# Moving lays to ScalarE, a third row rectified ahead, fp32 dummies and an earlier weight slot in an attention and spectral-mixing kernel

## The chip, the cores and the metric

The kernel runs on one core of a Trainium2 chip. The metric is the device time of one execution in microseconds, the median of several runs. The profile is of one execution, taken by the hardware profiler; its times are in microseconds from the start of the span. The engines are PE (TensorE matmuls), PEld (TensorE weight loads), DVE (VectorE), ACT (ScalarE), POOL (GpSimd) and SP (SyncE, which here only issues the output stores). Transfers run on DMA engines that the profile shows as one mean share.

## The reference

The input is q, k, v of shape (8 batches, 8 heads, 576 positions, 64), 64 pairs of weight matrices w_r and w_i of 512 x 512, one for each Fourier mode, and one matrix w_ch of 512 x 512.

```python
scores = q @ k.T / sqrt(64), masked to 0 <= pos_q - pos_k < 64
x = softmax(scores) @ v                       # per batch: 576 x 512
X = rfft(x, axis=seq)[:, :64]                 # 64 modes are kept
Y[m] = X[m] @ (w_r[m] + 1j * w_i[m])          # complex, per mode
u = x + irfft(Y, n=576)
out = u + relu(u @ w_ch)                      # fp32, 8 x 576 x 512
```

## The kernel before

The work has three stages, one after another, and beneath them one stream of weight loads.

**Attention** (36 steps of a loop over w, lines 417 to 457). At the start TensorE runs dummy matmuls (`warm_up`, line 369, bf16 128x512 on a tile of zeros) between the first transposes. Each batch's q, k and v are loaded raw, transposed on TensorE in twelve units (`transpose_units`, line 205), and attended in windows of 512 columns; the transposed v lies in the one tile `vT`. When a batch is attended, its rows go into `x_sb`, and TensorE makes its 64 Fourier modes (`dft`, `dft_turn`) into `XQ`.

**Modes** (lines 577 to 592 and 725 to 769). For each mode m TensorE multiplies `XQ` with w_r[m] and w_i[m] (lines 545 and 550). The 127 matrices, 512 KB each in bf16, are loaded by GpSimd's queue in order of use (`load_w`, line 110). GpSimd issues a load as soon as a place for it is free: the first 18 go to two weight pools, the next ones (`spare`, line 363) into tiles that attention no longer needs (raw tiles, kT, qT, vt, and, at step w = 36 of the loop, vT), and from then on a place is taken again when the mode that used it is done (`refill_w`, line 504). In the shadow of these loads `channel` (line 561) computes x @ w_ch for each of 36 row tiles into `Z0`. For each batch `spectrum` and `middle_rows` keep two things on up to 128 partitions, one for each real mode component: the mixed modes (`Yb`) and the mixed modes times w_ch (`yw`). The last four modes are done by `last` (line 751), each matrix as it lands, with dummy matmuls (`idle`, line 688, bf16 128x512) in between.

**Output** (lines 776 to 828). The last modes' rows come out of PSUM on ScalarE and VectorE into `yl`, and GpSimd's queue copies 8 rows for each further batch into that batch's `yw` and `Yb` (`send`, line 787). Then come 36 row tiles of 128 rows. Each takes one of eight PSUM banks in turn (`bank`, line 705) and goes through five steps:

1. lay (line 711): TensorE multiplies Z0's tile with the identity, which puts x @ w_ch into the bank;
2. rectify (line 808): TensorE adds the inverse transform of `yw`, ScalarE applies Relu in place;
3. finish (line 812): TensorE adds the inverse transform of `Yb`;
4. VectorE adds x and writes to `ot`;
5. SP issues the store.

The orders of PE, ACT, DVE, POOL and SP in this stage are those of the program text. Row n is rectified two rows ahead of the row being finished and laid four ahead; five rows are laid before the stage. A batch has 4.5 row tiles, so of each pair of batches nine tiles come, and the one with the two half rows (the pair tile) stands last of the nine. It needs two matmuls per add, and two stores.

Of the kernel before, what the change touches and what calls it, by code (L numbers as in the profile page):

```python
# [9 lines left out]
FP32 = mybir.dt.float32  # L10
FP32R = mybir.dt.float32r
BF16 = mybir.dt.bfloat16

ALU = mybir.AluOpType
# [6 lines left out]
def view(ap, off, dims):  # L21

    return bass.AP(ap.tensor, ap.offset + off, [list(ap.ap[0])] + [list(d) for d in dims])
# [3 lines left out]
def kernel(  # L27
# [10 lines left out]
    nc = tc.nc  # L38
    B, H, S, D = q.shape
    NM = moe_w_r.shape[0]  # L40
    DM = moe_w_ch.shape[0]
# [3 lines left out]
    NT = 5  # L45
# [22 lines left out]
    ident_bf = consts.tile([128, 128], BF16, name="ident_bf")  # L68
    ident_r = consts.tile([128, 128], FP32R, name="ident_r")
    x_sb = keep.tile([128, B, NT, DM], BF16, name="x_sb")  # L70
# [48 lines left out]
    warm = acons.tile([128, 512], BF16, name="warm")  # L119
# [29 lines left out]
    with tc.tile_pool(name="tmpf", bufs=1, side="right") as tmp:  # L149
# [8 lines left out]
        for t0, t1 in ((0, 3), (3, NT)):  # L158
            n = t1 - t0
            mt = tmp.tile([128, 2, n * NM], FP32, name="mtf")  # L160
            nc.vector.tensor_tensor(out=view(mt, 0, [[NM, n], [1, NM]]), in0=view(mo, 0, [[0, n], [1, NM]]),
                                    in1=view(to, t0, [[1, n], [0, NM]]), op=ALU.mult)
# [6 lines left out]
    vtp = p1.enter_context(tc.tile_pool(name="vtp", bufs=1, side="right"))  # L169
# [25 lines left out]
    pss = [ps_sc.tile([128, 512], FP32, name=f"pss{i}") for i in range(3)]  # L195
# [167 lines left out]
    def spare(t):  # L363

        nonlocal nw
        load_w(nw, None, None, view(t, 0, [[DM, NC], [1, DM]]))
        nw += 1

    def warm_up(n):
        for _ in range(n):  # L370
            nc.tensor.matmul(out=pss[2], lhsT=warm[:, 0:128], rhs=warm, start=True, stop=True)  # L371

    NU = 12

# [14 lines left out]
    dfts, turns = [], []  # L389
    NWIN = B * H * S // (2 * WIN)  # L390
    with tc.manual_schedule(engines={mybir.EngineType.PE, mybir.EngineType.Pool}):
        warm_up(14)
        first = transpose_units(0)
        for i, j in enumerate((0, 1, 2, 6, 7, 8, 3, 4, 5, 9, 10, 11)):
            first[j]()
            refill(0, j)
            if i in (2, 5):
                warm_up(6)
            if i in (6, 7, 8):
                warm_up(3)  # L400
        sched = {}

        for b in range(1, B):
            start = -(-9 * (b - 1) // 2)

            for i, j in enumerate(range(NU)):
                sched.setdefault(start + i // 3, []).append((b, j))
        units = {}
        mask(0, 1)

        def unit(b, j):
            if b not in units:
                units[b] = transpose_units(b)
            units[b][j]()
            refill(b, j)

        for w in range(NWIN + 1):
            todo = [lambda b=b: dft_turn(b) for b in turns]
            turns[:] = dfts
            todo += [lambda b=b: dft(b) for b in dfts]  # L420
            dfts.clear()
            todo += [lambda b=b, j=j: unit(b, j) for b, j in sched.get(w, [])]
            n = len(todo)
            if w < NWIN:
                scores(w)
            if w:
                cut = closes(w - 1)
                weigh(w - 1, 8 * w - 8, cut)
            if todo:
                todo.pop(0)()  # L430
            if w + 1 < NWIN:
                mask(w + 1, max(1, 3 - n))
            if todo:
                todo.pop(0)()
            if w:
                weigh(w - 1, cut, 8 * w)
            while todo:
                todo.pop(0)()

            if w in (NWIN - 4, NWIN - 1):  # L440
                i = (B - 2) % 2 if w == NWIN - 4 else (B - 1) % 2
                spare(kTs[i])
                spare(qtp.tile([128, 4, S], BF16, name="qT"))
            if w in (NWIN - 4, NWIN):
                i = (B - 2) % 2 if w == NWIN - 4 else (B - 1) % 2
                for j in range(2):
                    spare(vts[i][:, j])
                if w == NWIN - 4:
                    vt_mode = mode_of(nw - 1)
                if w == NWIN:  # L450
                    spare(vtp.tile([128, 4, S], BF16, name="vT"))
        for b in turns:
            dft_turn(b)
        for b in dfts:
            dft(b)
            dft_turn(b)
        early(EARLY)
# [11 lines left out]
    tiles = []  # L469
# [14 lines left out]
    Z0 = late2.tile([128, len(tiles), DM], FP32R, name="Z0")  # L484
    p2d = p2.enter_context(ExitStack())
    ps_a = p2d.enter_context(tc.tile_pool(name="ps_a", bufs=1, space=PSUM, reuse_waits="tile"))
# [69 lines left out]
    with ExitStack() as p2a:  # L556

        def channel_out(i):
            return Z0[:, i, :]
# [17 lines left out]
        for m in range(L0 * MG):  # L577
            mode(m)
            if m == 8:
                for b in range(1, B, 2):  # L580
                    tc.keep_in_program_order(nc.scalar.copy(out=x_sb[64:128, b - 1, NT - 1, :],
                                                            in_=x_sb[64:128, b, NT - 1, :]))
# [9 lines left out]
            if m == Z_M - 2:  # L592

                with tc.tile_pool(name="tmpi", bufs=1, reuse_waits="tile") as tmp:
# [21 lines left out]
                    for tab, row in ((trigI, pcol),):  # L616
# [23 lines left out]
                        for i in range(4):  # L640
# [7 lines left out]
                            for c0, c1, o in ((0, SW, i * SW),) if i < 3 else ((0, 80, 432), (80, SW, 576)):  # L648
                                nc.vector.scalar_tensor_tensor(
                                    out=tab[:, o:o + c1 - c0], in0=mt[:, c0:c1], scalar=coefc,  # L650
                                    in1=tis[:, c0:c1], op0=ALU.mult, op1=ALU.add)
# [33 lines left out]
        nc.vector.tensor_copy(out=pair_tile("Yb", b)[:E0], in_=psa[:E0].rearrange("p c e -> p (c e)"))  # L685
        nc.scalar.copy(out=pair_tile("yw", b)[:E0], in_=psw[:E0, :])

    def idle(n, pool=ps_a, tag="psw"):

        psd = pool.tile([128, DM], FP32, name="psd", tag=tag)  # L690
        for _ in range(n):
            nc.tensor.matmul(out=psd, lhsT=ident_bf, rhs=view(x_sb, 0, [[1, DM]]),
                             start=True, stop=True)

    seq = []
    for b in range(0, B, 2):
        seq += [(b + i, t) for i in range(2) for t in range(NT - 1)] + [(b, NT - 1)]
    NQ = len(seq)
    tps = {}
    taken = 0  # L700
# [4 lines left out]
    def bank(shape, dtype, name):  # L705
        nonlocal taken
        pool, tag = PLACES[taken % len(PLACES)]
        taken += 1
        return pool.tile(shape, dtype, name=name, tag=tag)

    def lay(n):
        ps = tps[n] = bank([128, DM], FP32, "pso8")
        nc.tensor.matmul(out=ps, lhsT=ident_r, rhs=channel_out(tiles.index(seq[n])), start=True, stop=False,  # L713
                         skip_group_check=True)

# [8 lines left out]
    with tc.manual_schedule(engines={mybir.EngineType.PE}):  # L724
        for m in range(M0, ME):
            if (m - M0) % 2 == 0 and (m - M0) // 2 < B // 2:
                b0 = m - M0
                mode(m, lambda: spectrum(b0))
                spectrum(b0 + 1)
            else:  # L730
                mode(m)
            if m == M0 + B - 2:
                wy = late.tile([128, 3, NC, DM], BF16, name="wy", tag="yt")
                free.extend([(wy, j, NM) for j in range(3)])
                refill_w(m)

        YT2 = wlate.tile([128, NC, 96], FP32R, name="YT2", tag="wl")
        nc.vector.tensor_copy(out=YT2[:, :, 0:R - RL], in_=YTl[:, :, 0, 0:R - RL])

        def middle_rows(b0, nb):  # L740
            psa = ps_a.tile([128, NC, 128], FP32R, name="psa", tag="psa")
            psw = ps_a.tile([128, DM], FP32, name="psw", tag="psw")
            turned(lambda e: view(YTl, (e * B + b0) * R, [[1, R * nb]]), R * nb, psa, psw)
            for i in range(nb):
                nc.vector.tensor_copy(out=pair_tile("Yb", b0 + i)[E0:],
                                      in_=psa[R * i:R * i + R].rearrange("p c e -> p (c e)"))
                nc.scalar.copy(out=pair_tile("yw", b0 + i)[E0:], in_=psw[R * i:R * i + R, :])

        psl = ps_l.tile([128, NC, RL * B], FP32, name="psl", tag="psl")

        def last(m, im):
            last_mode(m, wtiles.pop((m, im)), im, 0, NC)

        middle_rows(1, 4)
        last(ME, 0)
        lay(0)
        lay(1)
        last(ME, 1)
        middle_rows(5, 3)
        last(ME + 1, 0)  # L760
        for n in range(2, EARLY_ROWS):
            lay(n)
        idle(4)
        last(ME + 1, 1)
        for m in range(ME + 2, NM):
            for im in range(2):
                idle(6)
                last(m, im)
        idle(2)

    wl.close()
    p3 = p2.enter_context(ExitStack())
# [3 lines left out]
    with tc.manual_schedule(engines={mybir.EngineType.PE, mybir.EngineType.Activation, mybir.EngineType.DVE,  # L776
# [3 lines left out]
        psw = ps_a.tile([128, DM], FP32, name="psw", tag="psw")  # L780
        NR = R + RL * (B - 1)
        turned(lambda e: YT2[:, e, 0:NR], NR, psa, psw)
        idle(2, ps_l, "psl")
        flat = psa.rearrange("p c e -> p (c e)")
        yl = yp.tile([128, 2, DM], FP32R, name="yl")

# [25 lines left out]
        def finish(n):  # L812
            b, t = seq[n]
            add(n, "Yb", True)
            ot = op.tile([128, DM], FP32, name="ot")
            nc.vector.tensor_tensor(out=ot, in0=tps.pop(n), in1=x_sb[:, b, t, :], op=ALU.add)  # L816
            for i, (bb, r0, k) in enumerate(parts_of(b, t)):
                nc.sync.dma_start(out=out[bb, 128 * t:128 * t + k, :], in_=ot[r0:r0 + k, :])

        RELU = 2  # L820
        for n in range(RELU + 1):
            rectify(n)
        for n in range(NQ):
            finish(n)
            if RELU < n + RELU < NQ:
                rectify(n + RELU)
            if EARLY_ROWS <= n + RELU + 2 < NQ:
                lay(n + RELU + 2)


# [28 lines left out]
```

## Time and profile before

| | us |
|---|---|
| median of 4 runs (431.12 to 433.86) | 432.06 |
| profiled execution, its own time | 430.35 |
| span of the profiled execution | 428.6 |
| PE busy | 312.3 (73%) |
| DVE busy | 163.3 (38%) |
| ACT busy | 152.1 (35%) |
| last weight landed, first matmul on it | 391.47 |
| first Relu of the output stage | 395.05 |
| last VectorE sum, start | 422.63 |

The page gives busy shares in forty slices of 10.7 us, so a slice of the three stages can be told apart: attention to about 145 us, modes to about 391, output to the end. Busy shares over the whole span say little here, as the stages have different limits. In the chain of waits each piece of time is put down to the work that the next piece waited for.

### The profile page before, as it was taken

The numbers are of one execution on the slowest core, as the hardware profiler recorded it, in microseconds if no ns is written. First come the engines' busy times: TensorE is split into PE (matmuls) and PEld (weight loads), VectorE is DVE, ScalarE is ACT, GpSimd is POOL, SyncE is SP. The second block draws the span as 40 slices with busy tenths as digits, with TensorE's granted clock in tenths as the row PEclk, the third lists the DMA queues.
The fourth block names the chain that finished last, engine by engine and source line by source line (L and its number), as shares of the span: only waits on it lengthen the run. The fifth ranks groups of instructions, "written<-read, shape, count | busy, mean of one in ns | idle before, by whom it ended". The sixth has DMA issues, their size and how long they took to land.

```text
span 428.6 us, 11377 instructions
## 1 busy us (share of the span) xinstructions
PE 312.3 (73%) x5066; PEld 221.4 (52%) x5079; DVE 163.3 (38%) x316; ACT 152.1 (35%) x262; POOL 96.5 (23%) x184
## 2 busy tenths in 40 slices
PE   6989998999998766122678878776266762398994
PEld 2555765665665566122566656554244541354772
DVE  5465765766674100306222322221011110041994
ACT  4486765866864120101123222122011110032772
POOL 7131231331021404111211212211211032101500
PEclk9999999999999655555598988969556655589998
DMA  8999999999999999999999999999999999993897
GB/s 142 211 212 214 213 213 214 213 212 213 214 214 212 201 214 219 254 213 214 214 213 213 214 214 213 213 214 213 214 214 214 213 202 213 214 214 70 277 370 259
DMA packets 31089, 92.20 MB, mean 215 GB/s; under 512 B 3408, under 2 KB 3408, under 8 KB 31040
## 3 DMA queue, kind: packets, MB, share of 16 engines
q0 software_dynamic: 25792, 82.03, 96.3%
q1 hardware_dynamic: 5248, 9.44, 6.2%
q8 instruction: 40, 0.66, 0.6%
q14 instruction: 9, 0.07, 0.0%
HBM read 162.53 MB, written 9.44 MB: 401 GB/s over the span
## 4 chain that ended last, share of the span: by engine, by line
DMA 47%; PE 36%; DVE 6%; issue 5%; ACT 3%; POOL 2%; POOLq 0%; ACTq 0%
DMA wt<-in_moe_w_r_dram 30%; DMA wt<-in_moe_w_i_dram 17%; PE pso L316 6%; PE pst L218 6%; PE pso L805 4%; PE psv L235 3%; PE psx L338 2%; PE pss L272 2%; DVE x_sb L324 2%; PE pss L371 2%; PE pss L291 2%; PE psy L545 2%; PE psy L550 2%; DVE vT L59 2%; PE pso L713 2%
## 5 line engine op out<-in xcount | busy, mean ns | idle before, releaser
L550 PE MATMUL psy<-XQ,wt 128*128 128x16 bf16 x784 | 48.0, 191 | 47.3 <-DMA wt<-in_moe_w_i_dram 45.9
L545 PE MATMUL psy<-XQ,wt 128*128 128x16 bf16 x832 | 52.1, 191 | 33.5 <-DMA wt<-in_moe_w_r_dram 33.0
L550 PEld LDWEIGHTS <-wt 128*128 128x128 bf16 x784 | 37.3, 104 | 53.0 <-DMA wt<-in_moe_w_i_dram 51.2
L545 PEld LDWEIGHTS <-wt 128*128 128x128 bf16 x832 | 39.6, 104 | 38.5 <-DMA wt<-in_moe_w_r_dram 37.0
L115 POOL DMA_DIRECT2D wt<-in_moe_w_i_dram x51 | 27.6, 540 | 99.2 <-DMA wt<-in_moe_w_i_dram 40.8
L571 PE MATMUL psz<-wch,xT 128*128 128x512 f32 x144 | 47.0, 469 | 0.8 <-DVE xT L568 0.8
L115 POOL DMA_DIRECT2D wt<-in_moe_w_r_dram x55 | 29.6, 539 | 79.0 <-DMA wt<-in_moe_w_r_dram 38.8
L568 DVE CAST xT<-pxt 128x512 fp32r<-128x512 bf16 x36 | 23.5, 686 | 62.4 <-PE pxt L565 62.4
L573 ACT CAST Z<-psz 128x512 fp32r<-128x512 f32 x36 | 21.1, 586 | 69.8 <-PE psz L571 69.7
L297 ACT ACTIVATE et<-pss 128x512 bf16<-128x512 f32 x72 | 39.2, 600 | 12.2 <-PE pss L291 12.2
L316 PE MATMUL pso<-vt,et 128*64 128x65 bf16 (+1 forms) x576 | 32.8, 203 | 4.3 <-DVE x_sb L324 4.2
L571 PEld LDWEIGHTS psz<-wch,xT 128*128 128x128 f32 x144 | 29.8, 222 | 6.8 <-issue 1.1
L316 PEld LDWEIGHTS <-et 128*64 128x64 bf16 (+1 forms) x576 | 22.6, 109 | 15.7 <-issue 7.8
L324 DVE TENSOR_TENSOR x_sb<-pso,rcp 128x640 bf16<-128x640 f32 x32 | 26.3, 821 | 0.9
L816 DVE TENSOR_TENSOR ot<-pso,x_sb 128x512 f32<-128x512 f32 x36 | 24.7, 691 | 3.1 <-PE pso L805 2.6
L59 DVE CAST YT<-psy 128x256 fp32r<-128x256 f32 x6 | 2.5, 422 | 59.9 <-PE psy L550 59.9
L810 ACT ACTIVATE pso<-pso 128x512 f32<-128x512 f32 x36 | 20.8, 582 | 6.0 <-PE pso L805 3.4
L272 PE MATMUL pss<-band,ident_bf 64*64 64x512 bf16 x160 | 20.1, 391 | 1.6 <-ACT et L297 1.6
L58 ACT CAST YT<-psy 128x256 fp32r<-128x256 f32 x6 | 2.2, 373 | 52.7 <-DVE YT L59 52.7
L59 DVE COPY vT<-pst 128x768 bf16<-128x768 bf16 x16 | 15.3, 958 | 13.4 <-PE pst L218 13.4
L685 DVE CAST Yb<-psa 96x512 fp32r<-96x512 f32 x8 | 5.5, 687 | 31.5 <-PE psa L679 31.5
L677 PE MATMUL psw<-wch,YT 128*96 128x512 f32 (+1 forms) x36 | 17.0, 621 | 0.2 <-DVE YT L778 0.2
(164 smaller groups left out, 508.8 us busy)
## 6 DMA issues: line engine op xcount, KB each, us to landing
wt<-in_moe_w_r_dram POOLq DMA_DIRECT2D x55, 512.0 KB, 19.1
wt<-in_moe_w_i_dram POOLq DMA_DIRECT2D x51, 512.0 KB, 19.1
out_dram<-ot SPq DMA_DIRECT2D x32, 256.0 KB, 3.4
rk<-in_k_dram POOLq DMA_DIRECT2D x8, 576.0 KB, 9.2
rq<-in_q_dram POOLq DMA_DIRECT2D x8, 576.0 KB, 13.2
rv<-in_v_dram POOLq DMA_DIRECT2D x8, 576.0 KB, 11.8
wy<-in_moe_w_i_dram POOLq DMA_DIRECT2D x4, 512.0 KB, 16.5
kT<-in_moe_w_i_dram POOLq DMA_DIRECT2D x2, 512.0 KB, 7.8
```

The costliest lines, as they stand in the source:

```text
L59: return nc.vector.tensor_copy(out=o, in_=i)
L115: nc.gpsimd.dma_start(out=wt, in_=src[m].rearrange("(p c) e -> p c e", c=NC))
L218: nc.tensor.transpose(out=ps[64 * hh:64 * hh + 64, c, :], in_=src[:, hh, (c0 + c) * D:(c0 + c + 1) * D], identity=ident_bf)
L272: nc.tensor.matmul(out=pss[(2 * w + hh) % 3][64 * half:64 * half + 64, :], lhsT=ident_bf[pp, pp], rhs=view(band[pp], 128 * half, [[0, WIN ...
L297: nc.scalar.activation(out=et[:, hh, :], in_=pss[(2 * w + hh) % 3], func=ACT_F.Exp, scale=EX_SCALE)
L316: nc.tensor.matmul(out=pso[po, hh, (i // 2) * VW:(i // 2) * VW + D + 1], lhsT=et[pk, hh, col:col + 64], rhs=vt[pk, 1 - f % 2, 2 * hh + g / ...
L324: nc.vector.tensor_tensor(out=view(x_sb, b * NT * DM + g * D, [[4 * D, 2], [DM, NT], [1, D]]), in0=view(pso, 0, [[512, 2], [VW, NT], [1, D]]),
L545: nc.tensor.matmul(out=psy[:, m % MG, e, :], lhsT=wr[:, c, ee], rhs=XQ[:, c, :, 1:3, m], start=(c == 0), stop=(m == 0 and c == NC - 1))
L550: nc.tensor.matmul(out=psy[:, m % MG, e, :], lhsT=wi[:, c, ee], rhs=XQ[:, c, :, 0:2, m], start=False, stop=(c == NC - 1))
L568: nc.vector.tensor_copy(out=xT, in_=pst)
L571: nc.tensor.matmul(out=psz, lhsT=xT[:, c, :], rhs=wch[:, c, :], start=(c == 0), stop=(c == NC - 1))
L816: nc.vector.tensor_tensor(out=ot, in0=tps.pop(n), in1=x_sb[:, b, t, :], op=ALU.add)
```

## The change

Five edits are made together.

- Nine of the 36 row tiles (rows 11, 14, 16, 20, 23, 25, 29, 32 and 34) are laid by a ScalarE copy from Z0 into the bank, in place of the TensorE matmul. The first eight rows, and with them every bank's first use, stay on TensorE.
- Rows are rectified three ahead of the finished one, and laid five ahead. Row 5's lay moves to before the stage, to where two dummies stood.
- The pair tile comes sixth of its nine, and the last row is an ordinary one; its VectorE sum is cut into two halves of 256 columns, each with its own store, one on SP's queue and one on ScalarE's.
- The dummies become plain fp32 matmuls: the warm-up's 35 bf16 ones of 512 columns become 17 fp32 ones of 256 columns, and among the last modes one fp32 dummy stands for four bf16 ones.
- The place of vT is loaded with a weight matrix at step 31 of the attention loop and no longer at its end, ahead of kT, qT and vt. The matrices keep their order, so each following one moves by one place.

```diff
     def warm_up(n):
+        wide = warm.bitcast(FP32)
         for _ in range(n):
-            nc.tensor.matmul(out=pss[2], lhsT=warm[:, 0:128], rhs=warm, start=True, stop=True)
+            nc.tensor.matmul(out=pss[2][:, 0:256], lhsT=wide[:, 0:128], rhs=wide, start=True, stop=True)
...
-        warm_up(14)
+        warm_up(7)
...
             if i in (2, 5):
-                warm_up(6)
-            if i in (6, 7, 8):
                 warm_up(3)
+            if i in (6, 8):
+                warm_up(2)
...
+            if w == NWIN - 5:
+                spare(vtp.tile([128, 4, S], BF16, name="vT"))
...
-                if w == NWIN:
-                    spare(vtp.tile([128, 4, S], BF16, name="vT"))
...
-    def idle(n, pool=ps_a, tag="psw"):
-
-        psd = pool.tile([128, DM], FP32, name="psd", tag=tag)
-        for _ in range(n):
-            nc.tensor.matmul(out=psd, lhsT=ident_bf, rhs=view(x_sb, 0, [[1, DM]]),
+    def idle(wide, n):
+
+        psd = ps_a.tile([128, DM], FP32, name="psd", tag="psw")
+        for i in range(wide + n):
+            nc.tensor.matmul(out=psd, lhsT=ident_r.bitcast(FP32) if i < wide else ident_bf,
+                             rhs=Z0[:, 0, :].bitcast(FP32) if i < wide else view(x_sb, 0, [[1, DM]]),
                              start=True, stop=True)
...
-        seq += [(b + i, t) for i in range(2) for t in range(NT - 1)] + [(b, NT - 1)]
+        rows_of_pair = [(b + i, t) for i in range(2) for t in range(NT - 1)]
+        seq += rows_of_pair[:NT] + [(b, NT - 1)] + rows_of_pair[NT:]
...
     def lay(n):
         ps = tps[n] = bank([128, DM], FP32, "pso8")
+        if n >= NT + 4 and n % (2 * NT - 1) in (2, NT, NT + 2):
+            nc.scalar.copy(out=ps, in_=channel_out(tiles.index(seq[n])))
+            return
...
-        idle(4)
+        idle(1, 0)
         last(ME + 1, 1)
         for m in range(ME + 2, NM):
             for im in range(2):
-                idle(6)
+                idle(1, 2)
                 last(m, im)
-        idle(2)
+        idle(0, 2)
...
-        idle(2, ps_l, "psl")
+        lay(EARLY_ROWS)
...
-            nc.vector.tensor_tensor(out=ot, in0=tps.pop(n), in1=x_sb[:, b, t, :], op=ALU.add)
+            ps = tps.pop(n)
+            if n == NQ - 1:
+                for c0, queue in ((0, nc.sync), (DM // 2, nc.scalar)):
+                    cc = slice(c0, c0 + DM // 2)
+                    nc.vector.tensor_tensor(out=ot[:, cc], in0=ps[:, cc], in1=x_sb[:, b, t, cc], op=ALU.add)
+                    queue.dma_start(out=out[b, 128 * t:128 * t + 128, cc], in_=ot[:, cc])
+                return
+            nc.vector.tensor_tensor(out=ot, in0=ps, in1=x_sb[:, b, t, :], op=ALU.add)
...
-        RELU = 2
+        RELU = 3
...
-            if EARLY_ROWS <= n + RELU + 2 < NQ:
+            if EARLY_ROWS < n + RELU + 2 < NQ:
                 lay(n + RELU + 2)
```

## The prediction

> **What bounds the kernel now.** I read the page's forty slices first, then the chain that ended last, then the table of one-microsecond and five-microsecond stretches, and last the timeline of the output stage.
>
> ```profile
> PEclk9999999999999655555598988969556655589998
> DMA  8999999999999999999999999999999999993897
> GB/s 142 211 212 214 213 213 214 213 212 213 214 214 212 201 214 219 254 213 214 214 213 213 214 214 213 213 214 213 214 214 214 213 202 213 214 214 70 277 370 259
> ```
>
> The DMA row is full from slice 1 to slice 35: up to about 391 us the load stream sets the time, whatever the engines do. Slice 36 (386 to 396 us) is the hand-over, and the last three slices are the output stage. The chain agrees:
>
> ```profile
> 373.48 17.94 DMA wt<-in_moe_w_i_dram
> 391.47 0.66 PE psl L719 x16
> ...
> 403.42 0.48 PE pso L805 x2
> 403.90 0.23 PE pso L713
> ...
> 421.23 0.59 ACT pso L810
> 421.82 0.04 issue
> 421.86 0.75 PE pso L805 x2
> 422.61 0.02 issue
> 422.63 0.69 DVE ot L816
> ```
>
> It is DMA to 391.4 us, and then TensorE without a gap: per row two adds (L805) and one lay (L713). So there are two places where this change can count: the load stream before 391 us, and TensorE's order of work after it. The table by stretch (length, busy time of PE, PEld, DVE, ACT, POOL, then granted clock, DMA share, GB/s) shows both ends:
>
> ```profile
> 140.00:141.00 1.00, 0.60 (x18) 0.54 (x19) 0.33 (x2) 0.00 (x0) 0.03 (x1) 1.00 1.11 152
> ...
> 385.00:388.00 3.00, 2.69 (x26) 1.37 (x26) 0.00 (x0) 0.00 (x0) 0.00 (x0) 1.00 1.03 206
> 388.00:391.00 3.00, 2.39 (x25) 0.95 (x22) 0.00 (x0) 0.00 (x0) 0.00 (x0) 1.00 0.48 97
> ...
> 415.00:420.00 5.00, 5.00 (x23) 3.49 (x21) 4.71 (x7) 3.93 (x8) 0.00 (x0) 1.00 1.00 349
> ```
>
> See the 5.00 of 5.00 for PE at full clock, and the DMA share of 1.00 beside it: the output transfers are nearly a second bound. Then the rows that price a step, from the timeline:
>
> ```profile
> 395.05 1.56 ACT L810 ACTIVATE pso<-pso 128x512 f32<-128x512 f32 x3
> ...
> 397.20 0.19 PEld L805 LDWEIGHTS pso<-yw,trigI 128*128 128x128 f32 x1 [0.27 <-DMA yw<-yl]
> 397.21 0.49 PE L805 MATMUL pso<-yw,trigI 128*128 128x512 f32 x1
> ...
> 403.51 0.40 PE L805 MATMUL pso<-yw,trigI 128*128 128x512 f32 x1
> 403.74 0.40 PE L713 MATMUL pso<-Z,ident_r 128*128 128x512 f32 x1
> 403.98 0.39 PE L805 MATMUL pso<-Yb,trigI 128*128 128x512 f32 x1
> ```
>
> Matmuls of the output stage start 0.233 us apart and their result is there 0.40 us after the start; one that had to wait takes 0.49 and holds its successor back by 0.10. Three Relus in 1.56 us are 0.582 each, 0.489 from start to start.
>
> **The change, part by part.** The sum is made against the profiled execution: 430.35 us, its span 428.6 and 1.75 around it. The median shown, 432.06, lies 1.71 above that; I carry the shift over.
>
> *Nine lays by ScalarE.* They take 9 x 0.233 = 2.1 us of matmuls from TensorE and put nine copies on ScalarE, each queued right behind the Relu of the row two places earlier, and ahead of the next Relu. TensorE cannot add to the copied row before the copy ends. Count from the start of the first add of row r (its "rectify") to that of row r+2, the copied one. Before: add, lay, finishing add, add, lay, finishing add, six matmuls, 1.40 us. After: five, 1.17 us, but now row r+2's add needs add 0.40, hand-over 0.03, Relu of row r 0.58, gap 0.03, copy, hand-over 0.04. The trace has no copy from SBUF into PSUM of this size. Nearest rows: the 128x512 cast from PSUM to SBUF, 586 ns (L573), and the Relu, which overlaps its neighbour, 489 ns more per instruction; the 64x512 copy inside SBUF takes 611 (L581). I take 0.586, the plain copy of the same shape: 1.67 us, with the 0.10 for a matmul that waited 1.77, so 0.37 us more than before per copied row, 9 x 0.37 = +3.3. Ends: overlapped copy 0.489 and no gap, 1.64, +0.24 a row, +2.2; copy 0.611, +0.39 a row, +3.5. Behind the waiting add stand all further matmuls, VectorE's sums and the stores. The copies do not overload ScalarE (20.8 us of Relus in 30 us): it is the latency, not the load, that lands on the path.
>
> The Trainium skill, "ScalarE: Activation LUTs", section "What ACT_TABLE_LOAD costs", gives 186 ns plus 0.833 ns an element for such an instruction and an overlap of 93 ns between neighbours; the overlap is exactly the 582 less 489 of the Relu row. By it a copy would be 613 ns, 520 with the overlap, an estimate from that page, and the nine would cost +2.5 instead of my +3.3; the 586 of a measured copy without overlap stands in my sum.
>
> *Three ahead.* The first add of row 4 (batch 1's first) moves from 397.2 us to 396.5, since a rectify and no lay now stands before it. Its rows of yw come by a DMA issued at 395.36 that lands 1.8 us later, 397.17. So TensorE stands 0.7 there, +0.7 (ends 0.5 and 0.8); the finishing add of row 2 and VectorE wait behind it. The Relu itself had 1.17 us for 1.05 before, so the third step buys nothing in steady state; it saves the 0.36 us that the last-but-two finishing add waited at 419.87. Row 5's lay moves ahead of the stage in place of two dummies, where TensorE waits for ScalarE until 394.5 anyway: -0.2.
>
> *Pair tile mid-group.* The same matmuls in another place. What changes is the end: after the last Relu one finishing add of 0.50 instead of two of 0.75, -0.25. With the 0.36 above, -0.6. SP's two half stores move with it; SP's 40 issues remain, plus one on ScalarE's queue, which is then empty.
>
> *Last row in halves.* A 128x256 cast takes 0.42 (L59) against 0.69 for 128x512, so two overlapping halves end 0.1 later than one. But the last store now goes at once; before, SP issued the first half tile at 423.35 and the second at 423.88, 0.55 after VectorE's end: -0.5. That last store took 2.8 us to land with the share at 1.0; the very first one, unloaded, 2.5. Rows slower than before leave the queue emptier: -0.2 (0 to -0.3).
>
> *vT place five steps earlier.* One more load is queued at about 126 us, once TensorE's last read of vT (125.9) is over; GpSimd's 0.55 us for it fits before its next issue at 126.84, which waits for TensorE anyway. It fills the dip of 139 to 142 us, where 131 KB are missing against 213 GB/s, 0.6 us. I take 0 for it. The loads issued at 126.8, 127.6, 130.7, 131.3, 138.8 and 139.4 landed at 135.7, 138.2, 140.5, 143.1, 145.6 and 148.0, an even 2.5 apart, dip or not; and at the end the share falls to 0.48 for 388 to 391: about half the engines finish 3 us before the others. The dip emptied the early half; the late half sets the end. Ends 0 and -0.6. The one later load that waits for such a place (162.94) has loads queued until 167.7 before it.
>
> *Dummies and warm-up.* Hidden at both places if the clock holds. The warm-up feeds the attention stage, whose delays vanish under the load stream. Among the last loads, which land 2.2 to 2.5 us apart, 16 matmuls take 0.64 and two bf16 dummies 0.47, so the fp32 one may take 1.3 us before it delays anything; an fp32r matmul of that shape takes 0.233, the slowest 128x512 row (half clock) 0.43. I take 0. A short fp32 dummy would instead leave TensorE idler, and the clock is then the price (rival two).
>
> The Trainium skill, "Perfetto Trace Analysis", section "Engine Utilization", halves the array's output rate for its fp32 low-high mode; by it one fp32 dummy does the work of two bf16 ones and not of the four that it replaces, which speaks against this edit: TensorE would be less busy before the output stage, a cost of none or of rival two. No row of this trace shows a plain fp32 matmul.
>
> **Sum.** +3.3 +0.7 -0.2 -0.6 +0.1 -0.5 -0.2 = +2.6: span 431.2, profiled 432.95, median 434.7. With all low ends together +0.6 (432.7), with the high ones +3.1 (435.2).
>
> **Rivals.** *One, not slower: the copies are hidden.* If ScalarE's copy ended before TensorE came to the row, the nine lays would be a plain saving of 2.1 instead of +3.3 and the sum -2.8. The stores cap that: summed over 398 to 426 us their share is 27.5 us of 28, and no stretch holds over about 1.03, so at most 1.3 us can go: 430.8, with the dip's 0.6 also won 430.2. For it speaks that ScalarE is idle a quarter of the stage; against it the 1.17 us, of which 1.06 are gone before the copy starts: it decides only for a copy under about 0.1 us.
>
> *Two: the clock falls.* It has been full since 378 us, through the dummies (2.39 busy of 3.00 in the stretch above). At half clock a 128x512 matmul takes 0.43 instead of 0.233. High spells before lasted some 3.4 us; one such spell at half clock runs 8 matmuls instead of 14.6, 1.5 us lost, two 3.0: 437.7. It decides if the fp32 dummy keeps the array clearly less busy than four bf16 ones.
>
> *Three: the dip counts in full.* Then everything from 148 us on is 0.6 earlier: 434.1, still slower, but inside the half per cent.
>
> **How the numbers follow.** Half a per cent (2.16 us) is about what a measurement of this kernel can tell from no change. Forecast 0.62, rival one 0.16, rival two 0.08, rival three 0.14. The forecast's own range of 432.7 to 435.2 has two thirds of its weight above 434.2, so slower gets 0.41, rival two adds 0.08 and rival three 0.07 (its own spread): 0.56. Rival one with both gains and more than I count is the only way to faster, 0.08. Same is the rest, 0.36. The range runs from rival one without the dip, 430.8, to most of rival two, 437.0.
>
> **What would show it.** Right: TensorE idle before the first add of rows 11, 14, 16, 20, 23, 25, 29, 32 and 34, released by ScalarE's copy, some 0.4 to 0.5 us each; a wait of 0.7 for yw near 396.5; PE below 5.00 of 5.00 and the DMA share below 0.95 after 403 us; the last weight still landing near 391.4. Wrong: copies with no wait behind them, a last weight before 391.0, or a clock under 1 after 391 us.

## The result and the profile after

The changed kernel takes 433.41 us (median of 34 runs, 432.78 to 439.0), beside 430.92 us for the kernel before (53 runs). The ratio is 1.0056, 95% interval 1.0040 to 1.0071: slower by 2.4 us. The profiled execution took 432.78 us with a span of 431.0. A few executions of either kernel are some microseconds longer, and the ratio is that of the means, so it is not quite that of the medians.

The slices of the changed kernel:

```profile
PEclk9999999999995555555697989689565565599997
DMA  7999999999999999999999999999999999992986
GB/s 142 212 214 212 213 213 213 213 212 213 214 214 214 203 213 249 213 213 214 213 213 214 214 214 214 213 213 213 213 213 213 213 215 214 213 210 60 319 303 243
```

Up to slice 35 hardly anything has moved: the load stream is as full as it was, the dip near slice 13 is still there (203), and only the clock row is different in the middle, where the load stream hides it. The difference lies in the last four slices, so the four stretches shown for the kernel before are the next thing to look at (length, then busy time of PE, PEld, DVE, ACT, POOL, granted clock, DMA share, GB/s):

```profile
140.00:141.00 1.00, 1.00 (x25) 0.75 (x27) 0.00 (x0) 0.00 (x0) 0.00 (x0) 0.50 1.12 225
385.00:388.00 3.00, 3.00 (x24) 1.27 (x24) 0.00 (x0) 0.00 (x0) 0.00 (x0) 1.00 1.00 201
388.00:391.00 3.00, 2.29 (x21) 0.94 (x20) 0.00 (x0) 0.00 (x0) 0.00 (x0) 1.00 0.43 85
415.00:420.00 5.00, 4.58 (x19) 3.10 (x17) 3.88 (x7) 4.34 (x9) 0.00 (x0) 1.00 0.83 278
```

In the first line the dip of the load stream is not at 140 us any more (225 GB/s for 152): the attention ran at half clock from 130 us on here (before: from 142), the second load into kT was issued at 141.1 us in place of 138.8, and the dip came at 141 to 144 us (184, 143 and 188 GB/s). In the second, the new dummies keep TensorE busy 3.00 of 3.00, at full clock. In the third the share still falls before the last weight comes, as it did (0.48 before). In the fourth, TensorE now has 4.58 of 5.00 in place of 5.00, ScalarE 4.34 in place of 3.93, and the DMA share fell from 1.00 to 0.83. The chain of waits says what TensorE waits for:

```profile
395.15 1.79 DMA yw<-yl
396.94 0.04 issue
396.99 0.51 PE pso L811
...
400.98 0.47 PE pso L811 x2
401.48 0.58 ACT pso L816
402.06 0.51 ACT pso L717
402.57 0.04 issue
402.61 0.50 PE pso L811
403.11 0.23 PE pso L719
403.34 0.48 PE pso L811 x2
403.84 0.58 ACT pso L816
404.42 0.51 ACT pso L717
```

Where the chain of the kernel before was TensorE nearly all the way from 395.69 us, it now goes through ScalarE nine times: Relu (L816), copy (L717), hand-over, and then the add that waited. The timeline of one such place:

```profile
401.05 0.39 PE L811 MATMUL pso<-yw,trigI 128*128 128x512 f32 x1
...
401.97 0.58 ACT L717 COPY pso<-Z 128x512 f32<-128x512 f32 x1
401.98 0.40 PE L811 MATMUL pso<-Yb,trigI 128*128 128x512 f32 x1
402.48 1.94 ACT L816 ACTIVATE pso<-pso 128x512 f32<-128x512 f32 x3
402.61 0.19 PEld L811 LDWEIGHTS pso<-yw,trigI 128*128 128x128 f32 x1 [0.68 <-ACT pso L717]
402.61 0.50 PE L811 MATMUL pso<-yw,trigI 128*128 128x512 f32 x1 [0.24 <-ACT pso L717]
```

From the first add of one row (401.05) to that of the row two further, the copied one (402.61), pass 1.56 us, and 0.10 more for the matmul that had to wait: 1.66 against 1.40 before. The copy is 0.585 long, but it starts at 401.97, 0.09 before the Relu in front of it ends (402.06 in the chain above), and the Relu behind it starts at 402.48, 0.51 after the copy's start. The answers for the copy's line (median and the waits it caused, in us and times):

```profile
L717 ACT COPY pso<-Z x9: 584/585/585, 402.0 to 421.3; 128x512 f32<-128x512 f32 x9
...
  PEld pso L811: 6.1, 9
  PE pso L811: 2.2, 9
```

Nine copies, nine waits.

The last weight's first matmul comes at 391.26 here and 391.47 before, but from 391 to 396 in the profiles of the experiments below, so the output stage is compared from that matmul on. All times in this table are in us from it, out of the traces; "left" is what of the 9.44 MB of output (4.85 MB in e9) had not been stored when the last sum was done, from the DMA packets' records. These are single profiles: e4, whose output stage is that of the kernel before, ends its sums 0.03 us later and the kernel 0.26 later, so differences of this size in the column "end" say nothing.

| kernel | last sum done | left, MB | end | ratio, 95% interval |
|---|---|---|---|---|
| before | 31.85 | 0.88 | 37.11 | 1 |
| after | 34.24 | 0.92 | 39.74 | 1.0056 (1.0040 to 1.0071) |
| e1_no_copies | 31.86 | 1.11 | 37.67 | 0.9995 (0.9960 to 1.0030) |
| e2_copies_only | 33.75 | 0.68 | 38.81 | 1.0063 (1.0030 to 1.0096) |
| e3_three_ahead_only | 31.48 | 1.29 | 37.53 | 1.0008 (0.9978 to 1.0038) |
| e4_vT_place_only | 31.88 | 1.15 | 37.37 | 0.9978 (0.9948 to 1.0008) |
| e5_fp32_dummies_only | 32.98 | 0.78 | 38.53 | 1.0023 (1.0001 to 1.0044) |
| e6_copy_before_relu | 30.15 | 1.85 | 38.52 | 0.9994 (0.9962 to 1.0025) |
| e7_pair_order_and_halves | 31.71 | 1.25 | 38.22 | 1.0037 (1.0019 to 1.0055) |
| e8_two_store_queues | 30.14 | 1.88 | 39.54 | 1.0087 (1.0058 to 1.0117) |
| e9_half_stores | 30.16 | 0.59 | 34.65 | 0.9943 (0.9927 to 0.9959) |
| e12_copy_first_old_order | 30.09 | 1.84 | 37.38 | 0.9982 (0.9960 to 1.0005) |

### The profile page after: what moved, and what is told of

Read it like the earlier page. It is cut to its first block, busy times and chain, and to the rows that moved or that the text cites. A ratio compares the mean times of both kernels' runs of the same rounds, so it can differ in the third digit from the quotient of the medians.

```text
span 431.0 us, 11332 instructions
## 1 busy us (share of the span) xinstructions
PE 318.7 (74%) x5047; PEld 228.2 (53%) x5057; DVE 162.3 (38%) x317; ACT 155.8 (36%) x271; POOL 96.1 (22%) x184
## 3 DMA queue, kind: packets, MB, share of 16 engines
q1 hardware_dynamic: 5248, 9.31, 6.2%
HBM read 162.53 MB, written 9.44 MB: 399 GB/s over the span
## 4 chain that ended last, share of the span: by engine, by line
DMA 44%; PE 32%; issue 11%; DVE 6%; ACT 4%; POOL 1%; POOLq 0%; DVEq 0%; ACTq 0%
DMA wt<-in_moe_w_r_dram 32%; DMA wt<-in_moe_w_i_dram 11%; PE pso L316 6%; PE pst L218 5%; PE psv L235 3%; PE pso L811 3%; PE psx L338 3%; PE pss L272 2%; DVE x_sb L324 2%; PE pss L372 2%; PE pss L291 2%; PE psy L546 2%; PE psy L551 2%; DVE vT L59 2%; ACT pso L816 1%
## 5 line engine op out<-in xcount | busy, mean ns | idle before, releaser
L572 PE MATMUL psz<-wch,xT 128*128 128x512 f32 x144 | 48.4, 480 | 0.5 <-DVE xT L569 0.5
L316 PE MATMUL pso<-vt,et 128*64 128x65 bf16 (+1 forms) x576 | 34.4, 209 | 4.2 <-DVE x_sb L324 4.1
L316 PEld LDWEIGHTS <-et 128*64 128x64 bf16 (+1 forms) x576 | 23.9, 113 | 17.1 <-issue 9.0
L829 DVE TENSOR_TENSOR ot<-pso,x_sb 128x512 f32<-128x512 f32 x35 | 22.8, 687 | 6.7 <-PE pso L811 6.7
L272 PE MATMUL pss<-band,ident_bf 64*64 64x512 bf16 x160 | 21.2, 429 | 1.6 <-ACT et L297 1.6
L816 ACT ACTIVATE pso<-pso 128x512 f32<-128x512 f32 x36 | 20.6, 582 | 4.5 <-PE pso L811 3.2
L811 PE MATMUL pso<-yw,trigI 128*128 128x512 f32 x40 | 15.8, 423 | 2.8 <-ACT pso L717 2.2
```

What stands on the lines that cost most here:

```text
L272: nc.tensor.matmul(out=pss[(2 * w + hh) % 3][64 * half:64 * half + 64, :], lhsT=ident_bf[pp, pp], rhs=view(band[pp], 128 * half, [[0, WIN ...
L316: nc.tensor.matmul(out=pso[po, hh, (i // 2) * VW:(i // 2) * VW + D + 1], lhsT=et[pk, hh, col:col + 64], rhs=vt[pk, 1 - f % 2, 2 * hh + g / ...
L572: nc.tensor.matmul(out=psz, lhsT=xT[:, c, :], rhs=wch[:, c, :], start=(c == 0), stop=(c == NC - 1))
L811: nc.tensor.matmul(out=tps[n], lhsT=trigI[:, tr:tr + 128], rhs=pair_tile(what, bb), start=False, stop=stop and r0 + k == 128, skip_group_c ...
L816: nc.scalar.activation(out=tps[n], in_=tps[n], func=ACT_F.Relu)
```

## The experiments

The theory is that the nine copies cost the time, because TensorE waits for each behind a Relu. Its rivals: that another of the five edits costs it, or that the copies are hidden and the stores set the end.

**e1_no_copies**: the changed kernel with the copies taken out again.

```diff
-        if n >= NT + 4 and n % (2 * NT - 1) in (2, NT, NT + 2):
-            nc.scalar.copy(out=ps, in_=channel_out(tiles.index(seq[n])))
-            return
```

> All five edits, but the nine copied rows are laid by TensorE again. If the nine waits for a copy are what costs (0.26 us each by the trace of the changed kernel, 2.3 in all), the time falls from 433.4 to 430.6 to 431.3, a ratio to the kernel before of 0.999 to 1.001. If the loss sits in the wait for yw at the start (0.7 us) and in the row of stores at the end, it stays at 1.003 or above.

Measured: 431.77 us, ratio 0.9995; the ratio is as expected, the time is above the range named, as is that of the kernel before beside it (431.16). The first adds wait for no copy any more; of their idle time only the transfer of `yw` is left, in the groups of the output stage:

```profile
L808 PE MATMUL pso<-yw,trigI 128*128 128x512 f32 x40 | 14.9, 401 | 0.6 <-DMA yw<-yl 0.5
```

In the changed kernel the same line reads:

```profile
L811 PE MATMUL pso<-yw,trigI 128*128 128x512 f32 x40 | 15.8, 423 | 2.8 <-ACT pso L717 2.2 <-DMA yw<-yl 0.5
```

The last sum is back at 31.86, where it was before any change (31.85). So the copies hold the whole loss in the sums, 34.24 - 31.86 = 2.38 us.

**e2_copies_only**: the kernel before with those three lines added to `lay`.

> The kernel before with the nine copies as the only edit, two rows rectified ahead as there. If the latency of Relu and copy in line costs, +2.2 to +2.6 us, ratio 1.005 to 1.006; somewhat more, up to 1.010, if with two rows ahead the next Relu, now behind a copy, also holds up its finishing add. If the copies are harmless and something else in the change costs, 1.000, or below by the nine matmuls saved.

Measured: 434.64 us, ratio 1.0063; the last sum 1.90 us later than before. Taking the copies out and putting them in alone give about the same size (2.38 and 1.90 us in the sums), so the four other edits together are worth nothing that can be measured: e1's interval is 0.35% wide to either side. With only two rows ahead the wait is spread differently, as the expectation allowed: around 409.5 us of this profile the first add of a copied row starts 0.44 us after the matmul in front of it, and the finishing add behind that one, which waits for the next Relu, another 0.50, where 0.233 each would be the rule.

**e3_three_ahead_only**: the kernel before with a third row rectified ahead.

```diff
-        RELU = 2
+        RELU = 3
```

> The kernel before with three rows rectified ahead (and five laid ahead) as the only edit. By the prediction's terms +0.7 for the add that reaches batch 1 before its yw rows have landed, -0.4 for the wait near the end that goes: +0.3, ratio 1.000 to 1.002. If the third step hides a real wait in steady state, below 0.998.

Measured: ratio 1.0008, within what was expected, but the sums end 0.37 us earlier than before where 0.3 later was expected. The wait for `yw` comes with this edit, as predicted, here in the chain of waits and the timeline of this run:

```profile
398.16 1.79 DMA yw<-yl
```

```profile
399.99 0.51 PE L805 MATMUL pso<-yw,trigI 128*128 128x512 f32 x1 [0.52 <-DMA yw<-yl]
```

**e6_copy_before_relu**: the changed kernel, with each copy queued on ScalarE ahead of the Relu of the same step and not behind it. If the order on ScalarE's queue is what makes TensorE wait, the wait goes although the copies stay.

```diff
             finish(n)
+            far = n + RELU + 2
+            by_act = far >= NT + 4 and far % (2 * NT - 1) in (2, NT, NT + 2)
+            if far < NQ and by_act:
+                lay(far)
             if RELU < n + RELU < NQ:
                 rectify(n + RELU)
-            if EARLY_ROWS < n + RELU + 2 < NQ:
-                lay(n + RELU + 2)
+            if EARLY_ROWS < far < NQ and not by_act:
+                lay(far)
```

> All five edits, with one line moved: each of the nine copies is queued on ScalarE ahead of the Relu of the same step and not behind it, so ScalarE does it while it waits for TensorE's add. The work of every engine is that of the changed kernel. If it is the order (latency) that costs, TensorE's nine waits vanish and its 2.1 us of saved matmuls count: the time falls by 2.5 to 4 us, to 429.4 to 430.9, ratio 0.9965 to 1.000, with the stores as the floor. If it is ScalarE's load or its traffic into PSUM, the ratio stays at 1.004 or above.

Measured: 431.84 us, ratio 0.9994; the ratio is in the expected range, the time is not, and the kernel before took 431.16 beside it. The copy's line, its waits and two stretches near the end:

```profile
L717 ACT COPY pso<-Z x9: 586/614/632, 401.3 to 417.0; 128x512 f32<-128x512 f32 x9
...
  PEld pso L811: 0.6, 3
```

```profile
411.00:415.00 4.00, 4.00 (x19) 3.00 (x18) 3.67 (x7) 3.92 (x8) 0.00 (x0) 1.00 0.98 361
...
423.00:427.00 4.00, 0.00 (x0) 0.00 (x0) 0.00 (x0) 0.00 (x0) 0.00 (x0) 0.50 0.93 306
```

TensorE is busy 4.00 of 4.00 again, and as it has nine lays fewer, the last sum comes 4.1 us earlier than in the changed kernel and 1.7 earlier than in the kernel before. And yet the time is that of the kernel before: in the second stretch all compute is over and the DMA engines are still 0.93 busy, with 1.85 MB left at the last sum. The place of the copy in the queue is shown as the cause of the loss; what hides the gain is the stores, argued so far from the DMA share, and tested next.

**e9_half_stores**: e6 with half the columns stored.

```diff
-                nc.sync.dma_start(out=out[bb, 128 * t:128 * t + k, :], in_=ot[r0:r0 + k, :])
+                nc.sync.dma_start(out=out[bb, 128 * t:128 * t + k, 0:DM // 2], in_=ot[r0:r0 + k, 0:DM // 2])
```

> The kernel with the copies queued ahead of the Relu (e6_copy_before_relu), but every row but the last stores only its first 256 columns: half of the output is left unwritten, so that the stores are half as much. If the stream of stores is what took back the 1.7 us by which the last sum came earlier in e6, the end now follows the sums: from the first matmul on the last weight to the last sum 30 us, to the end 33 to 35 us, and the ratio is 0.988 to 0.995. If the stores are no limit and e6's time was set elsewhere, the ratio stays where e6 was, 0.998 to 1.001, with an end near 38 us.

Measured: 428.09 us, ratio 0.9943, and the end at 34.65: with less to store the end follows the sums, which did not move at all (30.16 against 30.15). Its stretches, the same two as for e6:

```profile
411.00:415.00 4.00, 4.00 (x19) 3.07 (x18) 3.68 (x6) 3.92 (x9) 0.00 (x0) 1.00 0.59 197
...
423.00:427.00 4.00, 0.00 (x0) 0.00 (x0) 0.00 (x0) 0.00 (x0) 0.00 (x0) 0.59 0.27 87
```

So in e6 the stream of stores is the bound, not TensorE.

**e8_two_store_queues**: e6 with every second row from row 13 on stored by GpSimd's queue.

```diff
-                nc.sync.dma_start(out=out[bb, 128 * t:128 * t + k, :], in_=ot[r0:r0 + k, :])
+                (nc.gpsimd if n > 11 and n % 2 else nc.sync).dma_start(
+                    out=out[bb, 128 * t:128 * t + k, :], in_=ot[r0:r0 + k, :])
```

> The kernel with the copies queued ahead of the Relu (e6_copy_before_relu), with every second row from row 13 on stored by GpSimd's queue in place of SyncE's. Two readings of the late stores in e6: if SyncE's issuing in a row is the limit, two queues take it away, the end comes about 5.3 us after the last sum (about 35.5 us from the first matmul on the last weight, against 38.52 in e6), and the ratio is 0.992 to 0.995. If the DMA engines themselves are full (their share was 0.98 to 1.03 in most stretches of e6), nothing is won: end 38 to 39 us, ratio 0.997 to 1.002, and the landing of each store gets longer by about what its issue gets shorter.

Measured: ratio 1.0087, worse than either reading. The last output packet was written 36.16 us after the first matmul on the last weight (36.04 in e6), so a second queue made the stores no faster: SyncE's issuing isn't the limit. That the DMA engines are fits the rest: their share is 0.99 to 1.02 from 407 to 427 us, and a full row's store takes 4.0 us (SyncE) or 5.2 us (GpSimd) from issue to landing, against 3.1 in e6. From that packet to the end it took 3.4 us against 2.5. That is 0.9 us of the loss; the medians of e8 and e6 stand 3.0 and 0.7 us above those of the kernel before beside them, and the rest of this difference stays open.

**e7_pair_order_and_halves**: the kernel before with only the new order of rows and the halved last row.

> The kernel before with only the order of rows changed (pair tile after five rows of the pair instead of last) and the last row's sum and store in two halves. By the prediction's terms for these two (-0.25 for the second add that the pair tile no longer makes at the end, +0.1 for the halves, -0.5 for the store issue, -0.2 for the landing; about -0.8 us together) the ratio is 0.998 and the span from the first matmul on the last weight to the end is about 36.3 us against 37.11 before. By the profile of the changed kernel, where SyncE's store queue was still behind when the last sum was done, the ratio is 1.000 to 1.001 and that span 37 us or more.

Measured: ratio 1.0037, more than both. The sums gained 0.14 us, as the prediction had it (-0.25 and +0.1), but the end came 1.1 us later. By 34 us 8.95 MB were stored, against 9.28 MB before (and 9.10 in e4, which has the old output stage). SyncE's queue was behind: the first half was ready at 422.84 in this profile, and SyncE issued its store at 424.27, after the stores of the two full rows in front of it. That the edits alone lose this, while e1, which holds them too, shows 0.9995, is just within the two intervals; how large the loss is stays open.

**e5_fp32_dummies_only**: the kernel before with only the dummies changed.

> The kernel before with only the dummies changed (fp32 ones, half as many or fewer). By the prediction they cost nothing: ratio 0.999 to 1.001, granted clock 1.00 in the stretch after the first matmul on the last weight, and TensorE's first transposes about 1.1 us earlier without effect on the last weight. By rival two, the clock falls in a gap that the dummies no longer cover: granted clock under 0.95 in a stretch of the output stage and a ratio of 1.003 or more.

Measured: ratio 1.0023, its interval's lower end at 1.0001. The granted clock is 1.00 in every stretch until TensorE has nothing left, so rival two isn't the reason. TensorE's first transposes come 0.2 us earlier, not 1.1. The profiled run shows another delay (a line of the chain of waits, then one of the timeline):

```profile
395.52 2.92 DMA yw<-yl
398.48 0.19 PEld L807 LDWEIGHTS pso<-yw,trigI 128*128 128x128 f32 x1 [1.38 <-DMA yw<-yl]
```

The small transfer into `yw` took 2.92 us from its issue and not 1.79, and the sums ended 1.1 us later. Of the eight profiles with these dummies it is late in two (2.92 here, 2.51 in e11) and takes 1.79 to 1.81 in the other six; in the six without them it takes 1.79 or 1.80. Whether the dummies or chance made it late is open.

**e4_vT_place_only**: the kernel before with only the place of vT given away earlier.

> The kernel before with only the place of vT given to the weights at step 31 of 36 in place of after step 36. By the prediction it is worth nothing: the last weight lands when it did, within the spread of 391.3 to 395.9 us that the runs show, ratio 0.9995 to 1.0005, and the dip in the DMA rate near 141 to 144 us stays or loses only its first half. By rival three the dip goes in full and the last weight comes 0.6 us earlier: ratio 0.9986.

Measured: 430.68 us against 431.41, ratio 0.9978, interval 0.9948 to 1.0008. This doesn't tell nothing from 0.6 us. The dip is still there, at 144 to 147 us (168, 82 and 184 GB/s).

**e10_one_pair_store** and **e11_copy_first_one_pair_store**: since the stores set the end, each pair tile goes out in one store of 128 rows and not in two of 64, in the kernel before and in e6.

```diff
-            for i, (bb, r0, k) in enumerate(parts_of(b, t)):
-                nc.sync.dma_start(out=out[bb, 128 * t:128 * t + k, :], in_=ot[r0:r0 + k, :])
+            if t == NT - 1:
+                nc.sync.dma_start(out=out[b:b + 2, 128 * t:128 * t + 64, :], in_=ot)
+            else:
+                nc.sync.dma_start(out=out[b, 128 * t:128 * t + 128, :], in_=ot)
```

> The kernel before, with each pair tile (64 rows of one batch, 64 of the next) stored by one DMA in place of two. In the profile of before the stores run near 380 GB/s, but fall to 190 to 270 GB/s for most of a microsecond after each pair tile (packets of 0.15 to 0.24 us in place of 0.09), about 130 KB lost each time, which is 0.35 us. If the two half-height stores cause this, the loss goes four times (-1.4 us) and one store issue goes at the end (-0.5 us): end 35.2 to 36 us after the first matmul on the last weight against 37.11, ratio 0.995 to 0.997. If the fall has another cause, only the last issue is saved: end 36.6 to 37.1, ratio 0.9985 to 1.000.

> The kernel with the copies queued ahead of the Relu (e6_copy_before_relu), with each pair tile stored by one DMA in place of two. There the sums end 1.7 us before those of before, and 1.85 MB of stores are left at that time, so what the stores gain is what the kernel gains: if the half-height stores cause the fall in rate, end about 1.4 us before e6's 38.52 after the first matmul on the last weight, ratio 0.995 to 0.997; if they don't, 0.998 to 1.001.

Measured: ratios 1.0357 and 1.0348, some 15 us lost by four stores. The end of e10 in stretches, and its DMA queue:

```profile
430.00:435.00 5.00, 0.00 (x0) 0.00 (x0) 0.00 (x0) 0.00 (x0) 0.00 (x0) 0.50 0.84 292
435.00:440.00 5.00, 0.00 (x0) 0.00 (x0) 0.00 (x0) 0.00 (x0) 0.00 (x0) 0.50 0.25 97
440.00:445.00 5.00, 0.00 (x0) 0.00 (x0) 0.00 (x0) 0.00 (x0) 0.00 (x0) 0.50 0.13 51
```

```profile
q1 hardware_dynamic: 5128, 9.44, 6.0%
```

Long after the last sum the share is 0.13, two engines of sixteen. The packets agree: 4608 of 2 KB carry the output in both kernels, and each store has besides them one packet of 4 bytes per engine it uses. The kernel before has 5248 packets, 40 stores x 16 more than 4608; e10 has 5128, 32 x 16 + 4 x 2. So a store whose target has an outer dimension of 2 ran on two engines. The question it was made for, whether half-height stores cause the fall in rate after each pair tile, is not answered by it.

**e12_copy_first_old_order**: e6 with the order of rows and the whole last row of the kernel before.

> The kernel with the copies queued ahead of the Relu (e6_copy_before_relu), with the order of rows and the whole last row of the kernel before (the new order and the halves alone gave 1.0037). If that loss and e6's time add up, the ratio is 0.996 to 0.998 and this is the fastest of the kernels run. If the stores have a floor that the kernel before already meets (about 342 KB a microsecond from 10 us after the first matmul on the last weight, 1.06 MB by then, 9.44 MB in all, and 2.3 us behind the last packet: 36.8 us), the end stays at 36.8 to 37.5 us from there and the ratio at 0.998 to 1.001, although the sums end near 30 to 31 us against 31.85.

Measured: 430.6 us against 431.1, ratio 0.9982, interval 0.9960 to 1.0005: with e4 the lowest of the kernels that store everything, and like e4 not told from no change. The sums end 1.8 us earlier than before and the end is no earlier, at 37.38, as the floor of the stores has it. A version that clearly beats the kernel before was not found.

## Why the prediction was right, and where not

The forecast was 2.6 us more than before, measured were 2.4. Of the level, 434.7 against 433.41, most is the base: the four runs shown had a median of 432.06, and 53 runs have 430.92. The sum came out this near by luck: the cause and the place were right, but two terms were off by about 0.9 us each, in opposite directions.

- *Nine lays by ScalarE, +3.3.* The mechanism is shown by e1, e2 and e6, row by row where it was announced. The size was wrong: 2.38 us in the sums. The mis-sized term is the copy without overlap, 0.586 with a gap of 0.03 before it: it starts 0.09 before the end of the Relu in front of it and adds 0.51, so a copied row costs 0.26 more and not 0.37. That is close to the prediction's low end (0.489, +2.2), and it is what the overlap in the Relu row already showed. The Trainium skill's rule ("ScalarE: Activation LUTs", "What ACT_TABLE_LOAD costs") gave, as an estimate, 520 ns and +2.5 by its overlap of 93 ns; the measurement sides with it and against the row that I chose. It had the length itself at 613 ns, where the run shows 585.
- *Three ahead, +0.7, -0.2, and -0.6 with the pair tile; halves +0.1: together 0.0 in the sums.* e1, which holds all of these, ends its sums at 31.86 against 31.85, but the terms didn't come out one by one. The wait for `yw` was seen in place: 0.52 us, and 0.10 for the matmul that waited. And yet e3, the third row alone, ended its sums 0.37 us earlier, where +0.7 and -0.36 make +0.3. The gain that was left out is at the start: before, the finishing adds of rows 0 and 1 start 0.38 and 0.26 us late, and with a third row in front of them only the first does, by 0.14. e7, the pair tile and the halves alone, gave -0.14 for the forecast -0.15. In e1 the last matmul ends 0.46 us before that of the kernel before (30.67 against 31.13), but the last full rows' sums on VectorE start 0.60 us apart there, so VectorE and no longer TensorE sets the last sum, and takes the gain back.
- *Store issue -0.5, landing -0.2.* The gain didn't come. From the last sum to the end it took 5.50 us against 5.26; whether that is a loss isn't told, as the kernels with the old end of the stage (e2, e4, e5) have 5.06 to 5.55. The step that failed took SyncE's queue for empty when the last sum is done, on the ground that slower rows leave it emptier. It was not: the last three full rows' sums start 0.60 us apart, and SyncE, still issuing the rows in front, got to the half that VectorE finished at 425.18 only at 425.99:

```profile
420.01 5.89 SPq L831 DMA_DIRECT2D out_dram<-ot  x8
425.99 0.41 SPq L827 DMA_DIRECT2D out_dram<-ot  x1
```

- *vT place, 0.* The number held: the last weight moved by 0.2 us. The reason given for it, that a dip only empties engines which are done early anyway, did not. The edit moved the dip here and in e4; in e1, which holds it too, there is none near 140 us, but one in slice 32 (181 GB/s). And the traces show that a dip is paid in full. By 380 us GpSimd's queue had moved 79.82 MB in the kernel before, 79.46 in e4 and 78.89 in e2, and the last load landed at 391.42, 393.12 and 395.81 us. At 213 GB/s the missing 0.36 and 0.93 MB are 1.7 and 4.4 us, which is how much later they are; the other profiles fit within 0.3 us, but for e3, whose 79.44 MB would give 393.2 and whose last load landed at 394.22. So most of the scatter in the start of the output stage is bytes missed earlier, and a filled dip should give rival three's 0.6 us; that is an estimate from these rows, and the ratio of e4 excludes neither 0 nor 0.6.
- *Dummies, 0.* The clock was full in every profile from the last weight to TensorE's last matmul, so rival two falls. The plain fp32 matmul runs as two instructions (the listing of the changed kernel's dummies; five calls):

```profile
L693 PE MATMUL psd<-Z,ident_r x10: 592/634/697, 381.3 to 389.8; 128*128 128x512 f32 x10
```

  The second starts 0.51 us after the first and what follows it 0.43 after that, so one dummy holds TensorE for 0.94 us; the bf16 dummies beside it start 0.216 apart, so four of them take 0.86. The halving that the prediction took from the Trainium skill ("Perfetto Trace Analysis", "Engine Utilization") would fit one of the two instructions; the call takes both, so it is a quarter, and TensorE did not get idler.
- *Rival one, the copies hidden.* It was said to need a copy under 0.1 us. e6 shows a second way that was missed: the same copy, queued one place earlier on ScalarE. Then the lays are indeed saved, and the cap by the stores that the rival named is real: in e6 and e12 the sums end 1.7 us earlier and the end comes no earlier (38.52 and 37.38 against 37.11). In these profiles it lies nearer than the 1.3 us allowed for, but the ratios, 0.9994 and 0.9982, reach down to 0.996 with their intervals and don't exclude a gain of 1.3 us.

## What to carry to other kernels

Work moved to an engine that is only half busy is not free if its result is queued behind something the receiver has just asked for: look at where in the queue it stands, and try one place earlier before giving it back. When two resources are both near full in a stage (here TensorE 5.00 of 5.00 and the DMA share 1.00), relieving the one gives at most the small gap to the other, so halve the other's work in an experiment to see how far it is. For the end of a kernel, price the last store with the queue in front of it, not with the queue empty.

## What the runs showed of the hardware

- A ScalarE copy of 128x512 fp32 from SBUF into PSUM takes 0.585 us (0.614 in e6) and overlaps its neighbours, so that it adds 0.51 between two Relus.
- A plain fp32 matmul of 128x512 takes two instructions, 0.94 us in all, a little over four times a bf16 one (0.216).
- The stores run at 342 KB per microsecond over 24 us of the output stage of the kernel before, and in no kernel that stored all of it clearly faster (343 at most, in e12); a second queue did not raise it.
- A store with an outer dimension of 2 in its target used two DMA engines, and four of them in 36 cost 15 us.
- The first of the 16 KB transfers into `yw` landed 1.8 us after its issue in twelve profiles, and 2.51 and 2.92 after it in two.
- The last of the loads landed between 391.2 and 395.8 us; in e2 and e4 the delay is what the megabytes not moved by 380 us take at 213 GB/s.
